# Loading q and k four heads at a time in rows of 6 KB, with heads paired one-and-three and two-and-four

## The chip, the cores and the metric

The kernel runs on one core of one Trainium2 chip. The metric is device time in microseconds of one execution; lower is better. A kernel's time is the median of several runs.

## What is computed

Two stages follow each other: causal attention in which some heads see everything and the others only a few sink positions and a window, and a soft mixture of experts over its output. The reference, cut to what matters:

```python
# q, k, v: (4, 8, 768, 64) float32; n_sink = 4, window = 64; is_retrieval: one flag a head
scores = q @ k.transpose(0, 1, 3, 2) / sqrt(64)
keep = causal                                  # retrieval heads
keep = causal & (is_sink | rel < window)       # the other heads
a = softmax(where(keep, scores, -1e9), axis=-1)
x = (a @ v).transpose(0, 2, 1, 3).reshape(3072, 512)     # tokens x (head, d)

logits = x @ phi                               # phi: (512, 32), 8 experts of 4 slots
slots = softmax(logits, axis=0).T @ x          # 32 x 512
for e in range(8):                             # w1: (8, 512, 1024), w2: (8, 1024, 512)
    slot_out[e] = maximum(slots[e] @ w1[e], 0) @ w2[e]
out = softmax(logits, axis=1) @ slot_out       # 3072 x 512 float32
```

## The kernel before

**Pairs.** The attention runs over 16 pairs of heads, `n` from 0 to 15: pair `n` is heads `2*(n%4)` and the next one, of batch `n//4`. A pair's two heads lie in the two halves of the 128 partitions. For each pair the loop body (lines 325 to 397) makes six chunks of scores (`scores`, line 160) on PE, the exponentials of each on ACT (line 172), masks on DVE (line 184), then the products with v of the pair before (`pvmm`, line 186) and their division into the token rows `xb` (`norm`, line 196). The instruction order on every engine is the order of the Python text: the kernel is under a manual schedule, and the pools only decide which buffer a tile gets and so what it has to wait for.

**q and k.** `load_qk` (line 106) fetches q and k from GpSimd's queue, with a cast to bf16 on the way, as rows of 12 tokens: partition `64*h + p` holds tokens `12*p` to `12*p + 11` of head `h`, 3 KB in the source and 1.5 KB in SBUF. Pairs 0 to 3 are loaded pair by pair, the others two pairs in one transfer, with the second pair beside the first in the row. The first q of all, `stage` (line 252), is issued from ACT's queue in float32 and cast by DVE (line 282). `transposes` (line 135) turns a pair's q or k with 24 small PE transposes, and `evac` (line 144) copies the result to `Tq` on DVE (line 148) or `Tk` on ACT (line 151). Pair 0 is turned ahead of the loop, pair 1 at the end of `n == 0`, and pair `n + 1` within iteration `n` for `n` from 1 to 14. The raw rows have two buffers (line 65), so a load waits until PE has turned what lay there.

**v and the weights.** `load_v` (line 116) fetches v of four heads in rows of 256 bytes, three buffers. `w_load` (line 128) spreads the loads of w1 (1 MB in bf16 each) and most of w2 over the loop. The last w2 loads take the place of tiles that attention uses to its end: `w2_5` (line 407) that of the masks, `w2_6` and `w2_7` (line 404, in halves) those of the exponentials. All of these, q, k, v and weights, go through GpSimd's queue in the order of the text.

**Experts.** After the loop the last pairs are finished, the slot sums of the four batches are added (`slot_bf`, line 461), and w1 and w2 are applied (lines 486, 526, 518). The columns are done in two halves: with the left half of expert 7's w2 the left half of the output begins, with the right half the rest (`product`, line 545), and the output is written in rows of 24 tokens a partition. `x` has its 512 columns in the order of the pairs: `norm` writes pair `n` into columns `128*(n%4)` onward, and `phi` and w1 are read in the matching order.

Of the kernel before, what the change touches and what calls it, by code (L numbers as in the profile page):

```python
# [10 lines left out]
F32 = mybir.dt.float32  # L11
# [7 lines left out]
NP = 16  # L19
# [19 lines left out]
def kernel(  # L39
# [24 lines left out]
    singles = ent(tc.tile_pool(name="singles", bufs=1))  # L64
    raw = ent(tc.tile_pool(name="raw", bufs=2))
    qkT = ent(tc.tile_pool(name="qkT", bufs=2))
# [8 lines left out]
    def single(shape, dt, name, tag=None):  # L75
        return singles.tile(shape, dt, name=name, tag=tag or name)
# [7 lines left out]
    sum4 = single([P, P], BF16, "sum4")  # L84
    expT = single([96, B, 256], BF16, "expT")
    colpart = single([96, B], F32, "colpart")
    rrow = single([P, 24], F32, "rrow")
    slot_acc = single([P, DM], F32, "slot_acc")
    slot_bf = single([P, DM], BF16, "slot_bf")
    xT = single([P, 4, S], BF16, "xT")  # L90
# [3 lines left out]
    siT = single([P, 4, ES], BF16, "siT")  # L94
    slot_out = single([P, DM], BF16, "slot_out")
    ri = single([1, 2 * H], I32, "ri")
# [6 lines left out]

    qraw, kraw, qT, kT, vf, pT, pv, xb = {}, {}, {}, {}, {}, {}, {}, {}

    def load_qk(pairs, order="qk"):
        b, h, c = pairs[0] // 4, 2 * (pairs[0] % 4), 2 * len(pairs)
        t = raw.tile([P, 2, 2, S], BF16, tag="raw", name="raw")
        for which in order:
            src, d, z = (q, qraw, 0) if which == "q" else (k, kraw, 1)  # L110
            nc.gpsimd.dma_start(t[:, z, :len(pairs)],  # L111
                                src[b, h:h + c].rearrange("(y h) (p s) d -> (h p) y (s d)", h=2, s=12))
            for x, n in enumerate(pairs):
                d[n] = t[:, z, x]

# [5 lines left out]
    def vb(n):  # L121
        return vbs[n // 2 % 3][:, 2 * (n % 2):2 * (n % 2) + 2]

# [10 lines left out]

    def transposes(n, which):
        src = (qraw if which == "q" else kraw)[n]
        tp = trp.tile([P, 12, 64], BF16, tag="tr", name="tp" + which)
        for s in range(12):
            for hh in range(2):
                po = slice(64 * hh, 64 * hh + 64)  # L140
                nc.tensor.transpose(tp[po, s, :], src[po, 64 * s:64 * s + 64], ident[po, po])  # L141
        return tp

    def evac(n, which, tp):
        dst = qkT.tile([P, S], BF16, tag="T" + which, name="T" + which)
        o, i = dst.rearrange("c (p s) -> c p s", s=12), tp.rearrange("c s p -> c p s")
        if which == "q":
            nc.vector.tensor_copy(o, i)  # L148
            qT[n] = dst
        else:  # L150
            nc.scalar.copy(o, i)  # L151
            kT[n] = dst

    def vfar(n):
        h = 2 * (n % 4)
        t = vfp.tile([P, 2, 4, 66], BF16, tag="vf", name="vf")
        nc.vector.tensor_mul(t, vb(n)[:, :, :4, :], fmask[:, h:h + 2])
        vf[n] = t

    def scores(n, c):  # L160
        o, ln, parts = CHUNKS[c]
        sc = scp.tile([P, 2, 512], F32, tag="sc", name="sc")
        at = 0
        for j, i0, cnt in parts:
            for hh in range(2):
                po = 64 * hh
                nc.tensor.matmul(sc[:, hh, at:at + 128 * cnt], kT[n][po:po + 64, j * 128:(j + 1) * 128],  # L167
                                 qT[n][po:po + 64, i0 * 128:(i0 + cnt) * 128], start=True, stop=True)
            at += 128 * cnt
        if c == 0:  # L170
            pT[n] = ptp.tile([P, 2, NPT], BF16, tag="pT", name="pT")
        nc.scalar.activation(pT[n][:, :, o:o + ln], sc[:, :, :ln], ACT.Exp, scale=scale)  # L172

    def mask(n, c):
        h = 2 * (n % 4)
        if c == 0:
            x, m = pT[n][:, :, 0:512], msk[:, h:h + 2, 0:512]
        elif c == 1:
            x = pT[n][:, :, 512:1024].rearrange("p h (a c) -> p h a c", a=2)
            m0 = msk[:, h:h + 2, 256:512]  # L180
            m = bass.AP(tensor=m0.tensor, offset=m0.offset, ap=[m0.ap[0], m0.ap[1], [0, 2], [1, 256]])
        else:
            x, m = pT[n][:, :, 1024:1408], msk[:, h:h + 2, 256:640]
        nc.vector.tensor_mul(x, x, m)  # L184
# [56 lines left out]
    def slot_sum(b):  # L241
# [3 lines left out]
        else:  # L245
# [5 lines left out]
    stage = ptp.tile([P, S], F32, tag="pT", name="stage")  # L251
    nc.scalar.dma_start(stage, q[0, 0:2].rearrange("h (p s) d -> (h p) (s d)", s=12))
    t0 = raw.tile([P, 2, 2, S], BF16, tag="raw", name="raw")
    qraw[0], kraw[0] = t0[:, 0, 0], t0[:, 1, 0]
    nc.gpsimd.dma_start(kraw[0], k[0, 0:2].rearrange("h (p s) d -> (h p) (s d)", s=12))
    diff = single([P, 256], F32, "diff")
    nc.gpsimd.iota(diff, pattern=[[1, 256]], base=0, channel_multiplier=-1,
                   allow_small_or_imprecise_dtypes=True)
    load_qk([1])
    load_v(0)  # L260
    nc.gpsimd.dma_start(w1s[0], w1v[0])

# [14 lines left out]
    sk2 = single([P, 1], F32, "sk2")  # L277
    ge = single([P, 256], BF16, "ge")
    grade = single([P, 640], BF16, "grade")
    V.tensor_single_scalar(rne, ri.rearrange("p (h c) -> p h c", c=2), 0.0, op=ALU.not_equal)  # L280
    V.tensor_tensor(rrow1, rne[:, :, 0], rne[:, :, 1], op=ALU.max)
    V.tensor_copy(qraw[0], stage)
    rb = trp.tile([P, H], F32, tag="tr", name="rb")
# [12 lines left out]
    def head_mask(h):  # L296
        V.tensor_scalar(msk[:, h], grade, thr[:, h:h + 1], None, op0=ALU.is_ge)

    for which in ("k", "q"):
        evac(0, which, transposes(0, which))  # L300
    for h in range(2):
        head_mask(h)
    def far_mask(n):
        h = 2 * n
        V.tensor_copy(fmask[:, h:h + 2, 1:], r1[:, h:h + 2].rearrange("p (h a d) -> p h a d", a=1, d=1).to_broadcast([P, 2, 3, 66]))
        V.tensor_copy(fmask[:, h:h + 2, 0], r0[:, h:h + 2].rearrange("p (h d) -> p h d", d=1).to_broadcast([P, 2, 66]))

# [17 lines left out]
    for n in range(NP):  # L325
        if n == 0:
            load_qk([2])
            load_v(1)
        elif n == 1:
            load_qk([3])  # L330
        elif n == 2 or (n % 2 == 1 and n < 12):
            m = 2 if n == 2 else (n + 3) // 2
            load_qk([2 * m, 2 * m + 1])
            load_v(m)
        w_load(1 + 5 * (n + 1) // 8)
        if n == 0:
            nc.gpsimd.dma_start(phi, moe_phi.rearrange("(do di) s -> di do s", di=P))
        b, r = n // 4 - 1, n % 4
        last = n - 1

        scores(n, 0)
        if n >= 1:
            for i in range(3):
                pvmm(last, i)
        if b >= 0 and r == 2:
            logits_mm(b, (0, 1, 2, 3))

        scores(n, 1)
        if b >= 0 and r == 2:
            logits_exp(b)  # L350
        if n >= 1:
            norm(last, 0)
        if 0 < n < NP - 1:
            tq = transposes(n + 1, "q")
            evac(n + 1, "q", tq)
        mask(n, 0)
        if b >= 0 and r == 3:
            exp_tokens(b)

        scores(n, 2)  # L360
        if n >= 1:
            pvmm(last, 3)
        if n >= 2:
            x_transpose(n - 2)
        mask(n, 1)

        scores(n, 3)
        if 0 < n < NP - 1:
            tk = transposes(n + 1, "k")
        mask(n, 2)  # L370

        scores(n, 4)
        if 0 < n < NP - 1:
            evac(n + 1, "k", tk)
        if n >= 1:
            pvmm(last, 4)
        if n:
            vfar(n)

        scores(n, 5)  # L380
        if n == 0:
            vfar(0)
        if n >= 1:
            pvmm(last, 5)
            norm(last, 1)
        if b >= 0 and r == 3:
            dispatch_mm(b)
            slot_sum(b)
        if n == 0:
            evac(1, "q", transposes(1, "q"))  # L390
            evac(1, "k", transposes(1, "k"))
        if n < 3:
            far_mask(n + 1)
            for h in (2 * n + 2, 2 * n + 3):
                head_mask(h)
        elif n == 3:
            setup_late()


# [60 lines left out]
    copies(4, 0)  # L460
    V.tensor_add(slot_bf, slot_acc, sps[bl][0])
    copies(5, 0)
# [90 lines left out]
    def half_rows(cs, t0, groups, banks, eng):  # L553
        ot, r = single([P, NL, 256], F32, f"oh{t0}", tag=f"w1_{t0}"), 0
        for rows in groups:
# [3 lines left out]
            eng.dma_start(ov[:, r - rows:r, cs], ot[:, r - rows:r])  # L559

    V.tensor_copy(slot_out[:, left], sp[0])  # L561
    half_rows(left, 0, (2, 2, 4), (1, 2), nc.gpsimd)
# [52 lines left out]
```

## Time and profile before

| | |
|---|---|
| median of 3 runs | 156.32 us (156.28 to 157.13) |
| the profiled execution | 156.77 us, of which 155.0 us lie between its first and last instruction |
| PE busy | 119.2 us (77%) |
| DVE busy | 108.0 us (70%) |
| ACT busy | 109.9 us (71%) |
| GpSimd's DMA queue | 27.10 MB in 35984 packets |
| mean granted PE clock | 0.899 |

The times of one execution in this text are counted from the first instruction. The 1.77 us by which the profiled execution is longer than its span lie outside the first and last instruction. The page slices the span into 40 equal parts (3.9 us each) and shows busy tenths for each engine; a GpSimd row "DMA_DIRECT2D" is the making of a transfer's descriptors, and the time to its landing is told separately.

### The profile page before, as it was taken

Reading aid. Unit: us, or ns where it says so; the run is one execution under the profiler, and the core shown is the slowest. Engines: PE = TensorE matmul, PEld = TensorE weight load, DVE = VectorE, ACT = ScalarE, POOL = GpSimd, SP = SyncE. Lnnn points to the kernel's source line nnn. Section 1 sums busy time; section 2 is a strip of 40 time slices with the busy share of each in tenths; the row PEclk is TensorE's granted clock in tenths of the full one; section 3 lists DMA queues with packets and bytes.
Section 4 is the critical chain, followed back from the end, with each engine's and each line's share of the span. In section 5 each row is a group of like instructions: output and inputs, shape, how many; then the busy total and the mean of one; then the engine's idle time right before and its main releaser. Section 6 shows DMA issues by size and latency. Waiting matters only on the chain. (4 is left out here: it accounts for less than half of the span.)

```text
span 155.0 us, 5046 instructions
## 1 busy us (share of the span) xinstructions
PE 119.2 (77%) x2237; PEld 74.8 (48%) x2239; DVE 108.0 (70%) x246; ACT 109.9 (71%) x147; POOL 38.7 (25%) x54
## 2 busy tenths in 40 slices
PE   6557787888597979977979979778987988789300
PEld 2234455555464655755656556455632466334200
DVE  2985679999987869979769879687745410539600
ACT  3248789889799999999898999999442420439600
POOL 7471443720350160070075200000360000400000
PEclk9955579999999999999999999999999998558955
DMA  5999999999999999999999999999999999969995
GB/s 125 148 198 198 171 220 204 193 191 186 216 222 195 188 218 196 188 214 202 186 213 206 189 216 214 216 216 218 214 209 220 206 190 200 167 227 368 406 387 188
DMA packets 38071, 33.05 MB, mean 213 GB/s; under 512 B 26018, under 2 KB 35106, under 8 KB 35874
## 3 DMA queue, kind: packets, MB, share of 16 engines
q0 software_dynamic: 35984, 27.10, 112.5%
q1 hardware_dynamic: 1922, 5.24, 8.8%
q10 hardware_dynamic: 144, 0.39, 0.8%
q8 instruction: 17, 0.28, 0.7%
q14 instruction: 4, 0.03, 0.1%
HBM read 52.49 MB, written 6.29 MB: 379 GB/s over the span
## 5 line engine op out<-in xcount | busy, mean ns | idle before, releaser
L172 ACT ACTIVATE pT<-sc 128x1024 bf16<-128x1024 f32 (+1 forms) x96 | 83.4, 923 | 9.4 <-PE sc L167 8.5
L167 PE MATMUL sc<-Tq,Tk 64*128 64x256 bf16 (+3 forms) x320 | 36.8, 294 | 13.7 <-ACT Tk L151 10.5
L193 PEld LDWEIGHTS <-pT 128*128 128x128 bf16 x672 | 24.6, 98 | 11.9 <-issue 7.6
L184 DVE TENSOR_TENSOR pT<-pT,msk 128x1024 bf16<-128x1024 bf16 (+1 forms) x48 | 29.4, 639 | 0.2 <-ACT pT L172 0.2
L193 PE MATMUL pv<-vb,pT 128*128 128x65 bf16 x352 | 27.2, 195 | 0.3 <-DVE xb L202 0.3
L193 PE MATMUL pv<-vf,pT 128*128 128x65 bf16 x320 | 24.9, 196 | 0.0
L167 PEld LDWEIGHTS <-Tk 64*128 64x128 bf16 x320 | 11.5, 96 | 23.1 <-ACT Tk L151 13.1
L141 PEld LDWEIGHTS <-raw 64*64 64x64 bf16 x768 | 16.0, 115 | 11.1 <-issue 10.5
L202 DVE TENSOR_TENSOR xb<-pv,rs 128x384 bf16<-128x384 f32 x32 | 17.8, 557 | 1.1
L148 DVE COPY Tq<-tpq 128x768 bf16<-128x768 bf16 x16 | 15.3, 956 | 4.4 <-PE tpq L141 4.2
L111 POOL DMA_DIRECT2D raw<-in_q_dram x9 | 5.9, 651 | 49.8 <-PE tpk L141 46.7
L151 ACT COPY Tk<-tpk 128x768 bf16<-128x768 bf16 x16 | 12.9, 804 | 4.4 <-PE tpk L141 4.4
L201 DVE RECIPROCAL rs<-pv 128x6 f32<-128x6 f32 x32 | 6.2, 194 | 11.2 <-PE pv L193 11.1
L141 PE MATMUL tpk<-ident,raw 64*64 64x64 bf16 x384 | 9.6, 200 | 3.1 <-DVE Tq L148 2.5
L118 POOL DMA_DIRECT2D vb<-in_v_dram x8 | 11.6, 1452 | 1.0 <-issue 0.9
L141 PE MATMUL tpq<-ident,raw 64*64 64x64 bf16 x384 | 9.8, 202 | 1.2 <-DVE r L292 1.2
L547 PE MATMUL bank<-slot_out,expR 128*128 128x256 bf16 (+1 forms) x33 | 9.5, 410 | 1.2 <-DVE slot_out L561 0.5
L210 PE MATMUL tpx<-ident,xb 128*128 128x128 bf16 x96 | 8.1, 218 | 1.9 <-ACT expT L224 1.1
L211 DVE COPY xT<-tpx 128x768 bf16<-128x768 bf16 (+1 forms) x17 | 9.0, 529 | 0.8 <-PE tpx L210 0.8
L549 ACT ACTIVATE ot<-bank,rrow 128x512 f32<-128x512 f32 (+1 forms) x9 | 5.6, 665 | 3.8 <-PE bank L547 3.7
L547 PEld LDWEIGHTS <-expR 128*128 128x128 bf16 x33 | 4.9, 155 | 6.1 <-issue 5.0
L132 POOL DMA_DIRECT2D w<-in_moe_w_dram x12 | 6.6, 557 | 3.8 <-DMA raw<-in_q_dram 1.9
(89 smaller groups left out, 113.7 us busy)
## 6 DMA issues: line engine op xcount, KB each, us to landing
w<-in_moe_w_dram POOLq DMA_DIRECT2D x14, 1024.0 KB, 17.1
vb<-in_v_dram POOLq DMA_DIRECT2D x8, 384.0 KB, 11.8
out_dram<-ot SPq DMA_DIRECT2D x3, 1024.0 KB, 5.3
raw<-in_q_dram POOLq DMA_DIRECT2D x6, 384.0 KB, 9.5
raw<-in_k_dram POOLq DMA_DIRECT2D x6, 384.0 KB, 10.6
w<-in_moe_w_dram POOLq DMA_DIRECT2D x4, 512.0 KB, 19.3
out_dram<-oh SPq DMA_DIRECT2D x2, 512.0 KB, 7.2
raw<-in_k_dram POOLq DMA_DIRECT2D x4, 192.0 KB, 5.8
```

The costliest lines, as they stand in the source:

```text
L118: nc.gpsimd.dma_start(vbs[m % 3].rearrange("p h j d -> p (h j) d")[:, :, :D], v[b, h:h + 4].rearrange("h (j p) d -> p (h j) d", p=P))
L141: nc.tensor.transpose(tp[po, s, :], src[po, 64 * s:64 * s + 64], ident[po, po])
L148: nc.vector.tensor_copy(o, i)
L151: nc.scalar.copy(o, i)
L167: nc.tensor.matmul(sc[:, hh, at:at + 128 * cnt], kT[n][po:po + 64, j * 128:(j + 1) * 128], qT[n][po:po + 64, i0 * 128:(i0 + cnt) * 128], s ...
L172: nc.scalar.activation(pT[n][:, :, o:o + ln], sc[:, :, :ln], ACT.Exp, scale=scale)
L184: nc.vector.tensor_mul(x, x, m)
L193: nc.tensor.matmul(pv[n][:, i % 3, hh, :], pT[n][:, hh, o:o + 128], vv[:, hh, j, :D + 1], start=(j == 0), stop=(j == i))
L202: nc.vector.tensor_mul(xb[b][:, 3 * half:3 * half + 3, h * D:(h + 2) * D].rearrange("p i (h d) -> p i h d", h=2), pv[n][:, :, :, :64], rs. ...
L210: nc.tensor.transpose(tp[:, i * 128:(i + 1) * 128], xb[b][:, i, hp * 128:(hp + 1) * 128], ident)
L211: nc.vector.tensor_copy(xT[:, hp, i0 * 128:i1 * 128], tp[:, i0 * 128:i1 * 128])
L547: nc.tensor.matmul(op, er[r], slot_out[:, cs], start=True, stop=True)
```

## The change

q and k of all heads but the first four are loaded four heads in one transfer as rows of 24 tokens: partition `32*h + p` holds tokens `24*p` to `24*p + 23` of head `h`, 6 KB in the source and 3 KB in SBUF. The row's two halves (`x` 0 and 1) are turned separately. With 32 partitions a head, the two partition halves of a turned tile hold heads one and three of a group of four in the same columns, or two and four, so pairs are now heads `(h, h+2)`: pair 0 is heads 0 and 2, pair 1 is heads 1 and 3, and so on. Each turned half has half of the tokens of both pairs; `Tq` and `Tk` become tiles of four heads, and both halves must be turned before either pair's scores.

So turning is one iteration earlier: groups 2 to 7 are turned in iterations `2m-2` and `2m-1`; group 1's first half within `n == 1` and its second at the end of `n == 1`; iteration 14 turns nothing any more. The raw rows get a third buffer; room for it comes from setup tiles (`diff`, `ge`, `grade`) that share the place of tiles first used later (`slot_acc`, `slot_bf`, `expT`), and from `slot_out` in the place of `slot_bf`.

The first four heads keep rows of 3 KB and come pair by pair (`load_pair`, and `stage`); a pair's two heads are no longer neighbours in the source. As built, the source pattern of these four transfers (q and k of pairs 0 and 1) has 2 steps of one stride, 64 steps of another and then the row of 768 elements; before, it had 128 steps and the row.

In GpSimd's queue, group 1 is loaded before the first weights (`w1s[0]`) and v; v of group 2 comes in iteration 1; `phi` is loaded in four pieces with the order of its rows changed to suit the pairs, before group 2. At the end `slot_bf` is written by two additions over 256 columns that restore the order of the columns, in place of one over 512.

```diff
-    raw = ent(tc.tile_pool(name="raw", bufs=2))
+    raw = ent(tc.tile_pool(name="raw", bufs=3))
...
+    def heads(n):
+        h = 4 * (n % 4 // 2) + n % 2
+        return slice(h, h + 3, 2)
+
+    def load_pair(n, order="qk"):
         for which in order:
-            src, d, z = (q, qraw, 0) if which == "q" else (k, kraw, 1)
-            nc.gpsimd.dma_start(t[:, z, :len(pairs)],
-                                src[b, h:h + c].rearrange("(y h) (p s) d -> (h p) y (s d)", h=2, s=12))
-            for x, n in enumerate(pairs):
-                d[n] = t[:, z, x]
+            src, z = (q, 0) if which == "q" else (k, 1)
+            nc.gpsimd.dma_start(raws[0][:, z, n * S:(n + 1) * S],
+                                src[0, heads(n)].rearrange("h (p s) d -> h p (s d)", s=12))
+
+    def load_four(m):
+        b, h = m // 2, 4 * (m % 2)
+        raws[m] = raw.tile([P, 2, 2 * S], BF16, tag="raw", name="raw")
+        for z, src in enumerate((q, k)):
+            nc.gpsimd.dma_start(raws[m][:, z], src[b, h:h + 4].rearrange("h (p s) d -> (h p) (s d)", s=24))
...
-        dst = qkT.tile([P, S], BF16, tag="T" + which, name="T" + which)
-        o, i = dst.rearrange("c (p s) -> c p s", s=12), tp.rearrange("c s p -> c p s")
+        if x == 0:
+            TT[m, which] = qkT.tile([P, 2, S], BF16, tag="T" + which, name="T" + which)
+        dst, i = TT[m, which], tp.rearrange("c s p -> c p s")
+        if m == 0:
+            o = dst[:, x].rearrange("c (p s) -> c p s", s=12)
+        else:
+            o = dst.rearrange("c x (p s) -> c (x p) s", s=24)[:, :, 12 * x:12 * x + 12]
...
-    nc.scalar.dma_start(stage, q[0, 0:2].rearrange("h (p s) d -> (h p) (s d)", s=12))
-    t0 = raw.tile([P, 2, 2, S], BF16, tag="raw", name="raw")
-    qraw[0], kraw[0] = t0[:, 0, 0], t0[:, 1, 0]
-    nc.gpsimd.dma_start(kraw[0], k[0, 0:2].rearrange("h (p s) d -> (h p) (s d)", s=12))
+    nc.scalar.dma_start(stage, q[0, heads(0)].rearrange("h (p s) d -> h p (s d)", s=12))
+    raws[0] = raw.tile([P, 2, 2 * S], BF16, tag="raw", name="raw")
+    load_pair(0, "k")
...
-    load_qk([1])
+    load_pair(1)
     load_v(0)
-    nc.gpsimd.dma_start(w1s[0], w1v[0])
...
         if n == 0:
-            load_qk([2])
+            load_four(1)
+            nc.gpsimd.dma_start(w1s[0], w1v[0])
             load_v(1)
+            for a in range(2):
+                for g in range(2):
+                    nc.gpsimd.dma_start(phi[64 * g:64 * g + 64, 2 * a:2 * a + 2],
+                                        moe_phi.rearrange("(a g x d) s -> a g d x s", a=2, g=2, x=2)[a, g])
         elif n == 1:
-            load_qk([3])
-        elif n == 2 or (n % 2 == 1 and n < 12):
-            m = 2 if n == 2 else (n + 3) // 2
-            load_qk([2 * m, 2 * m + 1])
-            load_v(m)
+            load_four(2)
+            load_v(2)
+        elif n % 2 == 0 and n < 12:
+            load_four(n // 2 + 2)
+        elif n % 2 == 1 and n < 12:
+            load_v((n + 3) // 2)
...
+        m, x = (1, 0) if n == 1 else (n // 2 + 1, n % 2)
+        turns = 0 < n < NP - 2
...
-        if n == 0:
-            evac(1, "q", transposes(1, "q"))
-            evac(1, "k", transposes(1, "k"))
+        if n < 2:
+            for which in ("q", "k"):
+                evac(n, 1, which, transposes(n, 1, which))
...
-    V.tensor_add(slot_bf, slot_acc, sps[bl][0])
+    for a in range(2):
+        i = slice(256 * a, 256 * a + 256)
+        V.tensor_add(slot_bf[:, i].rearrange("p (g x d) -> p x g d", g=2, x=2),
+                     slot_acc[:, i].rearrange("p (x g d) -> p x g d", g=2, x=2),
+                     sps[bl][0][:, i].rearrange("p (x g d) -> p x g d", g=2, x=2))
```

## The prediction, made before the changed kernel ran

> **What bounds the kernel now.** I read the page first, then the chain that ended last, then PE's timeline at the end, then the first ten microseconds. The slices of the page come first: after the first slice the DMA engines are busy to the end of the weights, and the bytes hardly vary.
>
> ```profile
> PEclk9955579999999999999999999999999998558955
> DMA  5999999999999999999999999999999999969995
> ```
>
> The chain that ended last puts 23.5 us on the last weights; then the output runs. PE's timeline shows how closely the engines follow:
>
> ```profile
> 112.92 23.51 DMA w<-in_moe_w_dram x2
> ...
> 136.46 0.64 PE bank L518 x7
> ```
>
> ```profile
> 131.06 0.62 PE L518 MATMUL bank<-w,hT 128*32 128x256 bf16 x8 [0.61 <-DMA w<-in_moe_w_dram]
> 132.20 1.96 PE L547 MATMUL bank<-slot_out,expR 128*128 128x256 bf16 x8 [0.52 <-DVE slot_out L561]
> 134.09 0.62 PE L518 MATMUL bank<-w,hT 128*32 128x256 bf16 x8
> 135.04 1.06 PE L269 MATMUL bank<-zero 128*128 128x512 bf16 x2 [0.33 <-issue]
> 136.46 0.62 PE L518 MATMUL bank<-w,hT 128*32 128x256 bf16 x8 [0.36 <-DMA w<-in_moe_w_dram]
> ```
>
> Here PE waits only 0.61 and 0.36 us for the last two pieces of w2. So there are two chains, and the shorter one is only 1.0 us behind: the stream of transfers (last landing 114.67 + 21.8 = 136.4), and computing, which runs from the first exponentials through 16 pairs to the experts. A faster stream brings at most 1.0 us; whatever delays the attention by more than 1.0 us is paid in full, since there is no other stall to give it back: ACT, which sets a pair's period, has few gaps from 23 to 109 us, none over 1.2. So the start counts as much as the end:
>
> ```profile
> 3.80 1.48 DVE L282 CAST raw<-stage 128x768 bf16<-128x768 f32 x1 [0.69 <-DMA stage<-in_q_dram]
> ...
> 9.93 5.06 ACT L172 ACTIVATE pT<-sc 128x1024 bf16<-128x1024 f32 x6 [2.84 <-PE sc L167]
> ```
>
> DVE waits for the first q. Behind this cast, on DVE, stand all the mask preparations and the copy of `Tq`, so the scores keep their distance of 5.5 us to it (9.28 to 3.80). Each microsecond by which `stage` lands later is one by which the attention starts later.
>
> **How transfers spread over the engines.** The DMA view of the first 5 us, queue by queue (packets, MB, share of 16 engines), and the issues:
>
> ```profile
> q0 software_dynamic: 182, 0.26, 38.2%
> q10 hardware_dynamic: 144, 0.39, 25.3%
> q1 hardware_dynamic: 2, 0.00, 0.0%
> ...
> stage<-in_q_dram ACTq DMA_DIRECT2D x1, 384.0 KB, 3.0
> ...
> ri<-in_is_retrieval_dram SPq DMA_DIRECT2D x1, 0.1 KB
> ```
>
> `stage` alone is on q10: 144 packets, which is 128 rows and 16 more. `ri`, a single row, is alone on q1: 2 packets, one row and one more. I read the surplus as one closing packet for each engine that takes part: 16 where the pattern's outer count is 128, one where it is one. The pattern decides the spread. After the change the four first transfers have a source whose outer count is 2 (2 x 64 x 768); everything else keeps 128 or 64. The trace holds no outer count of 2, so I bound it: 16 engines (the rows number 128 as before) or 2 (the outer count). The two rows above agree with the outer count as well as with the number of rows, and no row excludes the second. In the changed program the count of 2 is nearer to `ri`'s 1 than to 128, and I take 2 for the transfer from ACT's queue. The trace shows no transfer of few rows on GpSimd's queue, and there I take 16, with 2 as a rival.
>
> The Trainium skill speaks against this change here: the page "DMA: Bandwidth & Descriptors", section "Rules for kernel authors", says that the slowest dimension of both patterns sets the number of engines, and an outermost one below 16 confines the whole transfer to at most that many. The trace agrees for the counts 128 and 1. The same page (section "Why a DMA increments its semaphore by 16 and not by 1") names an exception in which GpSimd's queue gives some direct copies all 16. By the rule with this exception the sum is the forecast; by the rule alone, with all four confined, it lies between the forecast and the rival at 170.3 below; by 16 engines throughout, 155.9.
>
> **The change part by part.** First the price of a 3 KB row on one engine. The landings of q and k of group 4:
>
> ```profile
> DMA to landing us min/median/max: 11.5/12.2/12.8
> ```
>
> Issued at 41.18 and 41.87, they land at 52.7 and 54.7, in the stream's order: 2.0 us for 256 such rows, 16 an engine, or 0.12 us a row. (From the share of q10, 25.3% of 16 x 5 us over 128 rows, it is 0.16 us.)
>
> (1) `stage` on two engines: 64 rows each in place of 8, so 56 x 0.12 = 6.7 us more (8.8 at 0.16). Those two engines also have GpSimd's rows: `k` of pair 0 and both of pair 1, 3 x 8 rows, 2.9 us if the queues take turns. At worst v's first load and `w1_0` (2.5 and 4.8 us by their steps in the stream) fall between, too. `stage` lands at 3.8 + 6.7 = 10.5 at the earliest; 13.4 with the three loads; 22.8 at the latest. I take 13.4, since these three are issued within 3 us and stand ahead of the others. Scores start 9.6 us later; and `k`, transposed ahead of `q`, is there by then.
>
> (2) Rows of 6 KB: 14 loads of four heads' worth, now 1.9 to 2.0 us each. Weights, whose rows are longest, take 4.8 us a MB (v of group 4 lands at 43.08 + 14.1 = 57.2, the next w at 44.50 + 17.5 = 62.0), so a load could not take less than 1.8 us. The gain lies between 0 and 0.15 a load; I take half of it: 14 x 0.07 = 1.0 us of the stream. `phi` in four pieces costs three issues more (0.77 us each at most on GpSimd, while the queue has `w1_0` and v to move) and 0 to 0.9 us of the stream, taken as 0.3. The stream alone gives -0.7.
>
> (3) The third buffer takes 49.8 us of waiting off GpSimd. Nothing is gained, since the stream was never empty behind these waits. Now `load_v` of group 3 and later is what GpSimd stops at, until the pair that used the buffer has gone through `pvmm`; the w and the next q and k are queued behind it. By the stream's own steps (1.9, 1.9, 2.5, 4.8 us for q, k, v, w), 8 to 11 us of transfers are then still outstanding, so the stream isn't empty. q and k are wanted one iteration earlier: group 2 lands at 24.6 and 26.5 by these steps, and was turned at 24.61 and 27.03 by iteration 2 (which comes later now); group 6 lands at 73.7 and 75.6 against 74.8 and 77.1. All in time, by 0.1 us at the least; if one is late, its lateness is a stall of the pair. `w1_0` is 4 us later and wanted only at 119.
>
> (4) Turning group 1's second half at the end of iteration 1, with nothing beside it. The like of it today is at the end of iteration 0:
>
> ```profile
> 15.50 0.80 ACT L151 COPY Tk<-tpk 128x768 bf16<-128x768 bf16 x1 [0.51 <-PE tpk L141]
> 17.00 1.02 ACT L172 ACTIVATE pT<-sc 128x1024 bf16<-128x1024 f32 x1 [0.71 <-PE sc L167]
> ```
>
> ACT idles 0.51 + 0.71 = 1.2 us; iteration 14 loses its copy of 0.8. Net +0.4.
>
> (5) `slot_bf` in two additions: 0.68 us for 512 columns today. Half of it and a start of about 0.15 (the shortest DVE rows) each: +0.15 on the path to the experts.
>
> (6) Copies of the turned tiles now write pieces of 24 bytes at twice the step. The nearest row is the scaled copy to `xb`, 557 ns for 384 elements against 956 for 768, so between 0 and +0.15 us for each of 14 copies; PSUM's reading order is the same as before, and I take 0 with 2.1 as its bound. Masks and v at every second head have the same rows in another order: nothing, and if they cost, DVE's gaps behind ACT hide it.
>
> **The sum.** Computing: +9.6 + 0.4 + 0.15, less the 1.0 us in which it no longer waits for w: +9.2 on the profiled 156.77, or 165.9. The runs' median lies 0.45 below that execution: **165.5**. The stream doesn't take its place: two engines have 56 rows more, +6.7 - 0.7 = +6.0. What is late next: w2_5 to w2_7, freed by the end of the attention at 118 to 123, against a stream which has work until about 120; covered, since experts are 9 us later too. Its own range, from 10.5 us to about 18 for `stage`, is 162.6 to 170.
>
> **Rivals.** *All four stay on 16 engines* (30%): stream -0.7, computing +0.55 - 1.0; the smaller gain decides, 156.77 - 0.45 - 0.4 = 155.9, no change. For it: 128 rows of the same length on the SBUF side. It gets faster than that only by (2)'s upper end and with computing ahead too, which the 1.0 us forbids. *`stage` and the first k on the same two engines* (16%): 128 rows there in place of 8 and 8, `stage` at 3.8 + 120 x 0.12 = 18.2, +14.4: 170.3. For it: one rule for all queues; against it: two queues need not pick the same pair. *Only GpSimd's three are on two engines* (9%): `k` lands at 5.6 + 6.7 = 12.3; scores follow 2.4 us after it (9.28 - 5.68, less the 1.22 that PE waited for DVE), so +5.4 and 161.3. The forecast has 45%.
>
> Measuring this kernel can tell about 1% (1.6 us) from no change. Faster by over 1%: 5%; within 1%: 22%; slower: 73% (the three slow cases, and 3% of the first rival with (6) at its bound). The range, 155.4 to 170.5, takes in the first rival and nearly all of the slow ones.
>
> **What would show it.** q10 with 130 packets instead of 144 and `stage` landing beyond 10 us prove (1); 144 and 3 us refute it and with it the forecast. First exponentials at 19.5 instead of 9.93. Last w2 pieces landed well ahead of PE's wait for them. ACT idle by 1.2 us near the end of iteration 1. Loads of 6 KB rows stepping by 1.85 us would confirm (2). A wait of `tpq` or `tpk` for a landing from pair 4 onward would show (3) wrong.

## The result, and the profile after

The changed kernel takes 166.24 us (median; 165.43 to 167.35), the kernel before took 156.72 in the runs beside it: a ratio of 1.061, 95% interval 1.053 to 1.069. The profiled execution of after took 165.43 us, with a span of 163.7 against 155.0. The forecast of 165.5 was met in size; the way to it was partly another, and part of the agreement is luck.

The page of after, its slices and the two queues in question:

```profile
PEclk9955555599999999999999999999999999779955
DMA  1699999799999999999999999999999999989995
GB/s 15 86 188 211 189 121 140 112 148 198 201 162 210 218 217 168 218 203 193 209 190 210 206 187 216 214 220 214 214 214 220 210 196 197 186 222 362 412 384 196
...
q0 software_dynamic: 36896, 27.11, 105.9%
...
q10 hardware_dynamic: 130, 0.39, 0.7%
```

q10, which carries `stage` alone, has 130 packets in place of 144: the same 128 rows and two more instead of sixteen. The slices show the loss at once: DMA starts at 1 and 6, with 15 and 86 GB/s in the first two slices of 4.1 us. The first five microseconds, queue by queue, and the issues in them with the time to landing:

```profile
q0 software_dynamic: 1678, 0.01, 17.8%
q10 hardware_dynamic: 33, 0.10, 7.2%
...
raw<-in_k_dram POOLq DMA_DIRECT2D x2, 192.0 KB, 17.0
vb<-in_v_dram POOLq DMA_DIRECT2D x1, 384.0 KB, 18.0
raw<-in_q_dram POOLq DMA_DIRECT2D x1, 192.0 KB, 16.7
```

Before, q10 had moved all of its 0.39 MB in this time, and q0 had 182 packets with 0.26 MB. Now q10 has a quarter, and q0 shows 1678 packets with 0.01 MB: nine times the packets, nearly no bytes. GpSimd's transfers too need 17 to 18 us from issue to landing, where they needed 4.6 to 7.7. What waits for them, by the timelines of DVE, PE and ACT:

```profile
16.08 0.56 DVE L286 CAST raw<-stage 128x768 bf16<-128x768 f32 x1 [12.40 <-DMA stage<-in_q_dram]
```

```profile
19.02 0.85 PE L144 MATMUL tpk<-ident,raw 64*64 64x64 bf16 x24 [13.54 <-DMA raw<-in_k_dram]
19.68 0.83 PE L144 MATMUL tpq<-ident,raw 64*64 64x64 bf16 x24
```

```profile
22.21 5.07 ACT L178 ACTIVATE pT<-sc 128x1024 bf16<-128x1024 f32 x6 [1.50 <-PE sc L173]
```

`stage` lands at 16.1 (before 3.8), k of pair 0 only at 19.0, so k is the last thing that the scores wait for; the first exponentials come at 22.21 against 9.93, 12.3 later. But k is the later of the two by little: DVE had its own work behind the cast of `stage` until 19.03. In the run below in which only `stage` is late, the exponentials follow its cast by 5.23 us; here they follow it by 6.13, so of the 12.3 us only 0.9 are k's. The end of the chain, and PE there:

```profile
125.34 20.46 DMA w<-in_moe_w_dram
145.80 0.04 issue
145.85 0.43 PE bank L537 x8
```

```profile
143.83 0.62 PE L537 MATMUL bank<-w,hT 128*32 128x256 bf16 x8
144.38 1.07 PE L273 MATMUL bank<-zero 128*128 128x512 bf16 x3
145.85 0.40 PE L537 MATMUL bank<-w,hT 128*32 128x256 bf16 x8 [0.40 <-DMA w<-in_moe_w_dram]
```

The stream still ends last: its last weights land at 145.80 (before 136.42, so +9.4), and PE waits 0.40 us for them, nearly the 0.36 of before (the 0.61 us for the piece ahead of them are gone): both chains went back by much the same amount. How the difference of the spans comes about, in us from each span's start (landings and first exponentials from the trace):

| | before | after | difference |
|---|---|---|---|
| first exponentials | 9.93 | 22.21 | +12.3 |
| end of the last exponentials | 109.82 | 120.51 | +10.7 |
| first v lands | 11.18 | 22.28 | +11.1 |
| last weights land | 136.42 | 145.80 | +9.4 |
| span | 155.0 | 163.7 | +8.7 |

Computing made up 1.6 us between the first and the last exponentials, the stream 1.7 between its first v and its last weights. The last 0.7 came after the last weights (18.6 before, 17.9 now), and go with the granted clock: in that stretch its mean was 0.76 where it had been 0.68, and PE took 6.83 us for the same 33 matmuls in place of 8.13 (99779955 at the end of the row, before 98558955). The same stretch took 17.7 us at a clock of 0.78 in the head-by-head kernel below, and 18.7 at 0.68 in the one with neighbours, so this is no gain of the change.

### The profile page after: what moved, and what is told of

Same layout as the page of the kernel before. It is cut to its first block, busy times and chain, and to the rows that moved or that the text cites. A ratio compares the mean times of both kernels' runs of the same rounds, so it can differ in the third digit from the quotient of the medians.

```text
span 163.7 us, 5041 instructions
## 1 busy us (share of the span) xinstructions
PE 118.4 (72%) x2239; PEld 76.3 (47%) x2239; DVE 106.1 (65%) x247; ACT 108.7 (66%) x147; POOL 37.9 (23%) x55
## 3 DMA queue, kind: packets, MB, share of 16 engines
q0 software_dynamic: 36896, 27.11, 105.9%
## 5 line engine op out<-in xcount | busy, mean ns | idle before, releaser
L178 ACT ACTIVATE pT<-sc 128x1024 bf16<-128x1024 f32 (+1 forms) x96 | 82.5, 939 | 7.2 <-PE sc L173 6.3
L173 PE MATMUL sc<-Tq,Tk 64*128 64x256 bf16 (+3 forms) x320 | 36.5, 292 | 12.4 <-ACT Tk L158 5.5
L173 PEld LDWEIGHTS <-Tk 64*128 64x128 bf16 x320 | 13.3, 95 | 21.1 <-issue 7.7
L566 PE MATMUL bank<-slot_out,expR 128*128 128x256 bf16 (+1 forms) x33 | 8.5, 353 | 1.5 <-DVE slot_out L581 0.5
L286 DVE CAST raw<-stage 128x768 bf16<-128x768 f32 x1 | 0.6, 560 | 12.4 <-DMA stage<-in_q_dram 12.4
## 6 DMA issues: line engine op xcount, KB each, us to landing
w<-in_moe_w_dram POOLq DMA_DIRECT2D x14, 1024.0 KB, 17.9
```

Source lines behind the costliest of these rows:

```text
L173: nc.tensor.matmul(sc[:, hh, at:at + 128 * cnt], kT[po:po + 64, j * 128:(j + 1) * 128], qT[po:po + 64, i0 * 128:(i0 + cnt) * 128], start=T ...
L566: nc.tensor.matmul(op, er[r], slot_out[:, cs], start=True, stop=True)
```

## The experiments

Theory: the four first transfers, with an outer count of 2, each run on two engines, `stage` and the first k on the same two; nothing else in the change matters beyond a microsecond. Rivals: only `stage` (the forecast) or only GpSimd's three are confined; it is the stride or the third dimension of the pattern and not its outer count; the rest of the change costs or gains more.

**All four transfers issued head by head**, 64 rows each (after, otherwise unchanged):

```diff
-            nc.gpsimd.dma_start(raws[0][:, z, n * S:(n + 1) * S],
-                                src[0, heads(n)].rearrange("h (p s) d -> h p (s d)", s=12))
+            for i in range(2):
+                nc.gpsimd.dma_start(raws[0][64 * i:64 * i + 64, z, n * S:(n + 1) * S],
+                                    src[0, heads(n).start + 2 * i].rearrange("(p s) d -> p (s d)", s=12))
...
-    nc.scalar.dma_start(stage, q[0, heads(0)].rearrange("h (p s) d -> h p (s d)", s=12))
+    for i in range(2):
+        nc.scalar.dma_start(stage[64 * i:64 * i + 64], q[0, 2 * i].rearrange("(p s) d -> p (s d)", s=12))
```

> The changed kernel with the first four transfers (q and k of pairs 0 and 1) issued head by head, so that the outermost count of each pattern is 64 and not 2; all else as changed. Theory: an outer count of 2 puts a transfer on two engines, and the four transfers alone cost the time. Then the first q lands near 4 us, the first exponentials start at 10 to 11 us, the stream of weights ends 1 to 2 us earlier than before the change, and the time is 153 to 156 us. Rival (the order of GpSimd's queue and phi in four pieces delay the start): 163 us or more, with q still landing after 10 us.

Measured: 157.62 us against 156.81, ratio 1.0044 (0.9999 to 1.0088). Nearly all of the 9.5 us is gone, so it lay in these four transfers. But the kernel isn't faster than before: the time of 153 to 156 us and the earlier weights were expected and did not come. The two lines from DVE's and ACT's timelines:

```profile
5.63 1.16 DVE L288 CAST raw<-stage 128x768 bf16<-128x768 f32 x1 [2.05 <-DMA stage<-in_q_dram]
```

```profile
11.26 5.06 ACT L179 ACTIVATE pT<-sc 128x1024 bf16<-128x1024 f32 x6 [3.83 <-PE sc L174]
```

The second half of `stage` lands only at 5.5, and the first v at 12.28 (+1.1), behind GpSimd's six issues where three stood; the last weights land at 137.07 (+0.65). (Fifteen of v's sixteen engines were through at 10.89, before at 10.74: one engine makes most of the 1.1 us, and what held it stays open.) Whether this or the rest of the change ate the gain was left to the last experiment.

**Only `stage`, or only GpSimd's three, head by head** (one half of the diff above each):

> Only the first q (from ACT's queue) is issued head by head; the other three start transfers keep the outer count of 2. Theory: the first k still has two engines to itself: 64 rows at 0.12 us, landing at 12 to 14 us, first exponentials at 15 to 17 us, 158 to 161 us. Rival (only ACT's transfer is confined; GpSimd's use all engines): first k at 6 us and 153 to 156 us.

> The first k, and q and k of pair 1, are issued head by head; the first q (from ACT's queue) keeps the outer count of 2. Theory: the first q has 64 rows on each of two engines, in turns with 24 rows a queue of GpSimd's: it lands at 11 to 15 us, first exponentials at 17 to 21 us, 159 to 164 us. Rival (only GpSimd's transfers are confined, and what ACT's waits for is their company): q at 4 to 5 us and 153 to 156 us.

Measured, one execution each: 162.80 and 163.35 us. With GpSimd's three confined, PE's wait for the first k:

```profile
12.40 0.85 PE L144 MATMUL tpk<-ident,raw 64*64 64x64 bf16 x24 [7.27 <-DMA raw<-in_k_dram]
```

With `stage` alone confined, DVE's wait for it:

```profile
14.43 0.56 DVE L287 CAST raw<-stage 128x768 bf16<-128x768 f32 x1 [10.85 <-DMA stage<-in_q_dram]
```

and, in the same run, PE's wait for DVE and ACT's first exponentials:

```profile
17.11 0.85 PE L145 MATMUL tpq<-ident,raw 64*64 64x64 bf16 x24 [7.54 <-DVE r L297]
```

```profile
19.66 5.07 ACT L179 ACTIVATE pT<-sc 128x1024 bf16<-128x1024 f32 x6 [9.26 <-PE sc L174]
```

Each alone costs 6 to 7 us; so both kinds of queue confine, against the forecast's assumption for GpSimd. Alone, k is there at 12.4 and `stage` at 14.4; together they are at 19.0 and 16.1. On different engines they would have kept those times: I read it as one pair shared by `stage` and the first k.

The records of after's trace bear this out. A transfer's semaphore, the counter that tells of its landing, is counted up by the engines as they get through with it. That of the first k shows fourteen counts at 3.91 to 4.07 us and the last two at 18.89 and 18.98; that of `stage` ends with two, at 15.82 and 16.05. And the packets of the two, from 6.4 to 15.5 us, come as two chains in which a row of `stage` and a row of k take turns, 0.246 us for both, where rows of `stage` alone had come every 0.118 us. The semaphores of GpSimd's other two transfers show their own slow pairs, at 13.21 and 13.36 and at 14.63 and 14.66, and yet end with two counts at 19.3 to 19.8, behind those of k.

v's first landing, which needs every engine, says the same: 11.18 before, 17.68 and 16.62 here (+6.5, +5.4), 22.28 with both (+11.1), which is nearly the sum. (The time of the first was 1.8 us above its range, though k and the first exponentials, 15.59, fell into theirs.)

**Only the strided sources in the kernel before**, heads 0 and 2, then 1 and 3, with everything else as it was; the same with the 64 rows outermost; and with four heads of 32 rows:

```diff
-    nc.scalar.dma_start(stage, q[0, 0:2].rearrange("h (p s) d -> (h p) (s d)", s=12))
+    nc.scalar.dma_start(stage, q[0, 0:3:2].rearrange("h (p s) d -> h p (s d)", s=12))
...
-    nc.scalar.dma_start(stage, q[0, 0:2].rearrange("h (p s) d -> (h p) (s d)", s=12))
+    nc.scalar.dma_start(stage, q[0, 0:3:2].rearrange("h (p s) d -> p h (s d)", s=12))
...
-    nc.scalar.dma_start(stage, q[0, 0:2].rearrange("h (p s) d -> (h p) (s d)", s=12))
+    nc.scalar.dma_start(stage, q[0, 0:8:2, :384].rearrange("h (p s) d -> h p (s d)", s=12))
```

> The kernel before, in which only the sources of the first four transfers take every second head (0 and 2, 1 and 3 in place of 0 and 1, 2 and 3), so that their outer count is 2; batch 0's attention is therefore that of other heads, and nothing else differs. Theory: this part of the change alone costs more than the whole: the first q lands at 15 to 17 us, the first k at 18 to 20 us, exponentials start at 21 to 23 us, and the time is 165 to 169 us. Rival (the start is late because of the new order of the queue): no more than 158 us.

> The kernel before with the same strided sources (heads 0 and 2, 1 and 3), the same rows and the same destinations, but with the order of the source's two outer dimensions exchanged: 64 rows outermost, the 2 heads within. So the rows of the two heads come alternately and batch 0's attention is not that of the reference; nothing else differs. Theory: the outer count alone decides, 64 puts the transfers on all engines: 144 packets on the queue of the first q, which lands near 4 us, and 156 to 158 us. Rival (the stride between heads, or a pattern of three dimensions, confines or slows them): q at 15 us and 165 to 169 us as with 2 outermost.

> The kernel before with sources of four heads and 32 rows each in the first four transfers, so that the outer count is 4 (batch 0's attention is that of other rows; nothing else differs). Theory: four engines a transfer, 32 rows on each: 132 packets on the queue of the first q, which lands at 7 to 8 us, the first k at 9.5 to 11 us, exponentials at 12 to 14 us, 158 to 161 us. Rival (2 is a special case and anything else uses all engines): 144 packets and 156 to 158 us.

Measured, one execution each: 168.16, 157.21 and 161.56 us. The page's rows of the two queues, in this order:

```profile
q0 software_dynamic: 38672, 27.11, 106.1%
...
q10 hardware_dynamic: 130, 0.39, 0.7%
```

```profile
q0 software_dynamic: 35984, 27.10, 112.4%
...
q10 hardware_dynamic: 144, 0.39, 0.8%
```

```profile
q0 software_dynamic: 37136, 27.11, 111.0%
...
q10 hardware_dynamic: 132, 0.39, 0.8%
```

and ACT's first exponentials:

```profile
22.38 2.64 ACT L172 ACTIVATE pT<-sc 128x1024 bf16<-128x1024 f32 x3 [1.50 <-PE sc L167]
```

```profile
9.89 5.07 ACT L172 ACTIVATE pT<-sc 128x1024 bf16<-128x1024 f32 x6 [3.05 <-PE sc L167]
```

```profile
16.01 5.07 ACT L172 ACTIVATE pT<-sc 128x1024 bf16<-128x1024 f32 x6 [1.50 <-PE sc L167]
```

The source patterns alone, without any other part of the change, give the whole loss (this one execution is even 1.9 us above the changed kernel's median). The same rows with the same strides in the order 64 x 2 cost nothing: it is not the stride, nor the three dimensions. An outer count of 4 gives 132 packets and about half of the delay (6.1 of 12.4 us). The surplus on q10 is 2, 16 and 4. So the outermost count decides. With four engines `stage` landed 1 us, and k 2 us, later than expected; the expectation had left out that these four, too, carry two transfers: the last four engines counted `stage` at 8.18 to 9.01 and the first k at 12.58 to 12.78.

**Rows of 3 KB again** in the head-by-head kernel (the row's halves 8 bytes apart in SBUF, so that they don't merge):

```diff
-        raws[m] = raw.tile([P, 2, 2 * S], BF16, tag="raw", name="raw")
+        raws[m] = raw.tile([P, 2, 2, S + 4], BF16, tag="raw", name="raw")
...
-            nc.gpsimd.dma_start(raws[m][:, z], src[b, h:h + 4].rearrange("h (p s) d -> (h p) (s d)", s=24))
+            nc.gpsimd.dma_start(raws[m][:, z, :, :S],
+                                src[b, h:h + 4].rearrange("h (p y s) d -> (h p) y (s d)", y=2, s=12))
```

> The kernel with the four start transfers issued head by head, and in addition the rows of q and k of groups 1 to 7 cut into two pieces of 3 KB (the row's two halves lie 8 bytes apart in SBUF); nothing else differs. Theory: the longer row is worth only some 0.04 us a load, so the steps of q and k in the stream go from 1.87 back to about 1.91 us, 0.6 us over 14 loads, and the time is 157 to 158.5 us. Rival (the rows of 6 KB are worth what was predicted, 1.0 us or more, and were lost elsewhere): steps of 1.94 us or more and 158 to 159.5 us.

Measured: 157.61 us against 156.62, ratio 1.0063 (1.0024 to 1.0103), where 6 KB rows gave 157.62 and 1.0044. Most loads of q or k step by 1.87 to 1.92 us here, by 1.83 to 1.89 in after, and by 1.80 to 1.93 in the head-by-head kernel, from which this one differs in the rows alone: at best 0.04 us a load, 0.5 us for fourteen, too little to see in the time.

**A version meant to gain**: head by head, but with the halves of `stage` issued from two queues, and the second group's q and k ahead of the first v:

```diff
+    for i, eng in enumerate((nc.scalar, nc.sync)):
+        eng.dma_start(stage[64 * i:64 * i + 64], q[0, 2 * i].rearrange("(p s) d -> p (s d)", s=12))
...
+    load_four(1)
     load_v(0)
```

> The four start transfers head by head as before, but the two halves of the first q from two queues (ACT's and SP's, ahead of the flags), and q and k of group 1 issued before the first v. Theory: what keeps the head-by-head kernel at the time of the kernel before is its start: 1.3 us for the second half of q behind the first on one queue, and 1.1 us of stream that waits for descriptors. Then the first q lands by 4.3 us, exponentials start at 9.9 to 10.4 us, the last weights land at 135.5 to 136.3 us, and the time is 155.0 to 156.5 us. Rival (the other parts of the change cost what the rest gains): no change against the head-by-head kernel, 156.8 to 158 us.

Measured: 157.06 us against 156.62, ratio 1.0061 (1.0028 to 1.0093); the expectation was missed. The first exponentials came at 11.08, hardly earlier than the 11.26 of the head-by-head kernel, and PE waited longer for weights:

```profile
131.58 0.62 PE L539 MATMUL bank<-w,hT 128*32 128x256 bf16 x8 [1.18 <-DMA w<-in_moe_w_dram]
...
136.83 0.62 PE L539 MATMUL bank<-w,hT 128*32 128x256 bf16 x8 [0.21 <-DMA w<-in_moe_w_dram]
```

The stream took some w steps of 5.2 to 5.9 us in place of 4.85; what made them long was not found, and the kernel before has two such steps as well (5.5).

**The first four heads as neighbours again**, the rest of the change kept. `heads(0)` and `heads(1)` become `slice(0, 2)` and `slice(2, 4)`, masks and v follow, and `norm` puts the columns where the rest expects them:

```diff
     def heads(n):
+        if n < 2:
+            return slice(2 * n, 2 * n + 2)
...
-                                src[0, heads(n)].rearrange("h (p s) d -> h p (s d)", s=12))
+                                src[0, heads(n)].rearrange("h (p s) d -> (h p) (s d)", s=12))
...
+            xb[b][:, 3 * half:3 * half + 3, :256].rearrange("p i (g x d) -> p i x g d", g=2, x=2)[:, :, n] if n < 2 else
...
-        if n >= 2:
+        if n == 3:
+            x_transpose(0)
+        if n >= 3:
             x_transpose(n - 2)
```

> The changed kernel, except that the first four heads of batch 0 go together as neighbours again (pair 0 is heads 0 and 1, pair 1 heads 2 and 3), so that the four first transfers are each one transfer with the same 128 rows outermost as in the kernel before; pairs 0 and 1 write their columns of x in the changed order, and pair 0's columns are turned an iteration later, in n == 3. Everything else of the change stays: rows of 6 KB, three raw buffers, the moved loads, phi in four pieces, slot_bf in two additions. Theory: the head-by-head kernel lost its 0.6 to 1.1 us to the descriptors of six small transfers on GpSimd, which made v's first load 1.1 us late; without them stage lands at 3.1 us, the first exponentials are at 9.9 to 10.0, v's first load lands at 11.2, and the last weights at 135.8 to 136.6 (14 loads at 0.04 us less, phi's pieces 0.4 us more): q10 has 144 packets, and the time is 155.9 to 156.9, the same as before within 1%. Rival: the 0.65 us at the end come from the rest of the change (phi in four pieces, w1_0 later, the third buffer); then the last weights land at 137 or later although v's first load is on time, and the time is 157.3 to 158.2.

Measured: 156.22 us against 156.36, ratio 0.9987 (0.9950 to 1.0024). The page's queues, ACT's first exponentials, the last weights in the chain and PE's wait for them:

```profile
q0 software_dynamic: 34208, 27.10, 111.3%
...
q10 hardware_dynamic: 144, 0.39, 0.7%
```

```profile
9.60 5.07 ACT L180 ACTIVATE pT<-sc 128x1024 bf16<-128x1024 f32 x6 [2.23 <-PE sc L175]
```

```profile
112.13 23.29 DMA w<-in_moe_w_dram x2
```

```profile
135.47 0.61 PE L542 MATMUL bank<-w,hT 128*32 128x256 bf16 x8 [0.57 <-DMA w<-in_moe_w_dram]
```

With one transfer each and 128 rows outermost the rest of the change costs nothing and gains nothing that can be measured: the last weights land at 135.42, 1.0 us before those of the kernel before in this one execution, and the median is 0.1 below. This is the best version of the change found, and it does not beat the kernel before. The head-by-head kernel's 0.8 us don't show here, which fits the six issues as their reason but does not prove it: v's first load lands at 11.68, earlier than the 12.28 there but not at the 11.2 expected, and the intervals of the two ratios overlap (from 0.9999 there, up to 1.0024 here).

## Why the prediction was right or wrong

- **Two chains, and a late start is paid: right; in full: wrong.** 12.3 us of late start became 10.7 at the end of the attention, 9.4 at the last weights and 8.7 in the span.
- **(1) The outer count sets the number of engines: right for `stage`, wrong for GpSimd's queue.** I took 16 engines for its three transfers, on an exception that the Trainium skill names for some of GpSimd's direct copies (page "DMA: Bandwidth & Descriptors", section "Why a DMA increments its semaphore by 16 and not by 1"); no row of before showed a transfer of few rows there. The runs do: k at 12.4 when GpSimd's three alone are confined, where it was at 5.7 before. The plain rule of that page's section "Rules for kernel authors" holds here for both kinds of queue. The forecast's own mechanism is the run with `stage` alone confined (GpSimd's loads head by head): there `stage` landed at 14.4 (forecast 13.4), the first exponentials at 19.66 (forecast 19.5), and the time was 163.4 (forecast 165.5). What happened was the 16% rival, one pair of engines for `stage` and the first k. So "`k` is there by then" is the step that failed: k came 2.9 us after `stage`.
- **The scores' distance to the cast of `stage` came out the same by luck.** 5.5 us were taken over from before, and after has 21.57 - 16.08 = 5.5. With `stage` alone late it is 19.01 - 14.43 = 4.6, since the cast itself takes 0.56 us in place of 1.48; k's lateness made up the 0.9.
- **That rival was over-priced** at 170.3: it had `stage` wait for all 128 rows on its pair (18.2, measured 16.1), while k came last (19.0). It took a start of +14.4 where +12.3 was measured, and gave nothing of it back. The forecast's number was met by luck, because its errors cancel: its start was 2.7 us too small (9.6 for 12.3); the attention gave back 1.6 us where the forecast had +0.4, an error of 2.0 the other way; and what follows the attention became 2.0 us shorter (45.2 before, 43.2 after) where it had 0.85, 1.2 more of that. Of these 2.0, 0.7 are the clock of this one execution.
- **The stream was to be off the critical path, with the last w2 pieces well ahead: wrong.** +6.0 was the rows of one transfer more on two engines; there were two transfers, +11.1 at the first v, and +9.4 at the end.
- **(2) Rows of 6 KB: too big.** At most 0.04 us a load, not 0.07; loads in after step by about 1.85, as predicted.
- **(3) The moved waits: right.** GpSimd's longest kinds of waits in after are at v, and before they were at raw:

```profile
POOL vb L121 <- PE pv L199: 27.2, 3, 9.2
```

  No turning waits for a landing from pair 4 on.
- **(4) Group 1's second half: right for the stall, and the attention as a whole wrong.** The idle time before the third pair is there, on ACT, 0.15 and 0.54 us where 1.2 was predicted:

```profile
34.51 0.81 ACT L158 COPY Tk<-tpk 128x768 bf16<-128x768 bf16 x1
...
35.97 0.80 ACT L158 COPY Tk<-tpk 128x768 bf16<-128x768 bf16 x1 [0.15 <-PE tpk L144]
37.31 3.56 ACT L178 ACTIVATE pT<-sc 128x1024 bf16<-128x1024 f32 x4 [0.54 <-DVE msk L301]
```

  Pair 2 starts 15.10 us after pair 0, before 14.05: +1.05. Iteration 14 became 1.03 shorter (0.8 predicted). But the other iterations together are 1.6 us shorter as well, iteration 2 by 0.7: the attention takes 98.30 us where +0.4 on 99.90 was forecast. In the two kernels with all first transfers on 16 engines it takes 98.87 (head by head) and 99.44 (neighbours, where iteration 3, in which pair 0's columns are turned as well, takes 7.47 us in place of 6.41); why the iterations in between are shorter was not separated.
- **(5) and (6), the smaller edits: not contradicted.** The neighbours' kernel has both and is no slower than before.
- **The first rival, 155.9 with 16 engines throughout, did not happen, but its sum agrees with the kernel with neighbours**, at 156.2; the interval there can't tell its gain of 0.4 us from nothing.

## What to carry to other kernels

A new order of heads or rows can change a transfer's outermost count from 128 to 2 with the same bytes, the same rows and the same destination, and then two engines move what sixteen did; look at the pattern as built, and at the queue's packets beyond its rows, which here gave the number of engines. Where a strided set of rows is wanted, put the long dimension outermost, issue it piece by piece, or choose a grouping whose first loads stay contiguous. A confined transfer delays everything behind it, since later landings need those engines too, and most where the first work of the kernel waits for it.

## What the runs showed of the hardware that was not expected

**Filler on the engines that are not used.** GpSimd's confined transfers put packets without a payload worth the name on the queue: 36896 against 34208 between after and the neighbours' kernel, 2688 more, which is 3 transfers x 14 idle engines x 64 rows. In the kernel before the strided sources add 38672 - 35984 = 2688 too, and with an outer count of 4 it is 37136 - 35984 = 1152 = 3 x 12 x 32. So each idle engine seems to get one for every row that a busy one gets. In the trace of after they carry 4 bytes and take 7 ns each (median).

**Other engines ran ahead without a landing.** In the third and fourth slice after moved 188 and 211 GB/s, as much as later, while of GpSimd's transfers nothing landed before 19.0 us; the slices from 20 to 37 us are lower (112 to 148). The engines that were free worked ahead in the queue: nine of the sixteen had counted the first v at 10.54 to 11.85, the last two at 22.15 and 22.28, and only then had it landed. Each landing waited for the slow pair.

**DVE beside the making of v's descriptors.** The same instruction on `diff` took 1.22 us in the neighbours' kernel, while GpSimd made the descriptors of v, and 0.29 in after, while GpSimd waited. From the timelines of the first and then of the second:

```profile
3.44 1.75 POOL L123 DMA_DIRECT2D vb<-in_v_dram  x1
```

```profile
4.05 1.22 DVE L292 TENSOR_SCALAR ge<-diff 128x256 bf16<-128x256 f32 x1
```

```profile
16.55 0.29 DVE L289 TENSOR_SCALAR ge<-diff 128x256 bf16<-128x256 f32 x1
```

In the kernel before it was the cast of `stage` that stood beside v's descriptors: 1.48 us, against 0.56 in after. But the neighbours' kernel has the cast at 0.56 inside the same 1.75 us, so not every instruction is held, and no run was made to tell what holds it.
